# Attention, maxout and bilinear layers on one core: weights of layers three and four in pieces, sums of y per tile

## The chip, the cores and the metric

One core of a Trainium2 chip runs the kernel. The metric is the device time of one execution in microseconds (us); three runs of the kernel before gave a median of 562.81 us (562.11 to 563.57). The engines are PE (matmuls; PEld is its weight load), DVE, ACT, POOL and SP, which here only issues DMAs.

## The reference

Three stages follow each other. The first is attention for 2 batches, 8 heads, 768 positions and 64 features: every query sees the keys within 15 positions and, beside them, 24 block summaries of the sequence.

```python
k_sum = k.reshape(B, H, nb, block, D).max(axis=3)      # block = 32
v_sum = v.reshape(B, H, nb, block, D).mean(axis=3)
scores_l = np.where(abs(pos_q - pos_k) < 16, scale * q @ k.T, -1e9)
scores_s = scale * q @ k_sum.T + log(block)
a = softmax(concat(scores_l, scores_s))
x = a @ concat(v, v_sum)                               # 1536 tokens x 512
h = maximum(maximum(x @ w1, x @ w2), x @ w3)           # layer one, 768 wide
y = h @ w_out                                          # layer two, 512 wide
out = ((y @ w_a) * (y @ w_b)) @ w_out2                 # layers three and four, 1536 wide
```

## The kernel before

The tokens are cut into four chunks of 384, `c` = 0 to 3; chunks 0 and 1 are the first batch, 2 and 3 the second. PE works in pairs of numbers: every operand is split into a rounded part and a remainder (`split`, L513, for activations; `w_parts`, L449, for weights), and a product is three matmuls (`mm3`, L508).

Weights come as 64-bit words in tiles of 128x512. For each, `w_load` (L415) issues a DMA on SP, `w_round` (L429) builds a 32-bit float with two ACT operations, a shift and an or on DVE (L445, L446) and an add on POOL (L447), and `w_split` (L455) makes the two parts with an ACT copy (L451) and a subtraction (L452, on DVE in this stage). Layer three multiplies 2x2 blocks by a seven-product scheme (`PRODUCTS`, L51). So for a pair of its tiles `w_split` also makes four half-width sums on DVE (L467 to L470) and splits two tiles of sums `s` and one quarter tile; and the activations need sums too, the T operands, which `sums_of` (L568) makes from the blocks of y with differences on DVE (`diff`, L581) and a copy and a subtraction for each operand (L578, L579). For chunks 2 and 3 `halves` (L562) calls it behind every second tile of y.

Layers one and two run chunk by chunk (`layers12`); attention of the second batch is laced into them. Then `layers34` runs `order34`: a0, b0, a1, o0, b1, a2, o1 and so on, with a and b the two factors of layer three for 256 features (`layer3`, 14 steps of six matmuls, seven products for each batch) and o layer four (`layer4`, 12 steps of six matmuls). Each step ends in a PSUM bank: qb, qg and qd in layer three, po in layer four, two buffers of each. Banks are emptied a step later by `evac`: ACT copies (L624, L632), adds on DVE (L634, L640), a multiply on DVE (L638) or POOL (L641), then a split into hg (L514 ACT, L515 DVE); in layer four an add on DVE (L681).

`weights(most)` (L480) traces up to `most` whole tiles' work for the next matrices as far as `fits` (L476) has room: room comes back when a layer's products are done (`w_freed`). At the end of the kernel it is called once for each step of `layers34`.

```python
for _ in layers34():
    weights(2)
```

Who runs when: a planner orders each engine's instructions by a simulated timeline, in which work traced earlier goes first among what is ready. `tc.issue_after(ins)` makes every instruction that the block traces on the engine of `ins` follow `ins` in that engine's queue; other engines' instructions are not bound. `mark[0]` is the last DVE instruction of that use. SP alone keeps the order in which its DMAs were traced (L80).

Of the kernel before, what the change touches and what calls it, by code (L numbers as in the profile page):

```python
# [9 lines left out]
F32 = mybir.dt.float32  # L10
# [4 lines left out]
AF = mybir.ActivationFunctionType  # L15
# [4 lines left out]
P = 128  # L20
# [32 lines left out]

W64, W32, WBUFS, QB, FB, SM, GB, BANKS = (4, 3), (4, 3), (24, 10), 4, (8, 2), 2, (12, 9), (2, 2, 1, 2, 2)

GATE, ROOM, SUMS, EARLY34 = (2, 3), 16, (46, 48, 50, 52), 6
LEAD, TURN, ERA0, ASKS, AHEAD, PRE, TURNS = 5, (11, 2, 2), 8, (3, 4, 5, 7, 9), (4, 1), 3, ((6, N1 - 6, 6, 4, 4, 8, N1 - 8, 4, 12), (24, 34), (34, 44))

# [10 lines left out]
def attention_then_maxout_then_bilinear(ctx: ExitStack, tc: tile.TileContext, qt, kt, vt, vwin, wall, const, out):  # L77
# [351 lines left out]
    def w_round(q):  # L429


        r = w64_t.pop(q).bitcast(U32).rearrange("p (n t) -> p n t", t=2)
        lw, hw = r[:, :, 0], r[:, :, 1]
        to = hw.bitcast(F32)
        if q < N12 + EARLY34:

            to = ps_c.tile([P, 512], F32, tag="c", name="psw")
        if BIAS_DVE[era(q)][q % 3]:
            V.tensor_scalar(to, hw.bitcast(F32), 2.0 ** -112, None, ALU.mult)
        else:  # L440
            A.activation(to, hw.bitcast(F32), AF.Copy, scale=2.0 ** -112)
        hw = to.bitcast(U32)
        A.activation(lw.bitcast(I32), lw, AF.Copy, scale=2.0 ** -29)  # L443
        w32_t[q] = w = w32_p.tile([P, 512], F32, tag=f"w32{q < N12}", name="w32", bufs=W32[q >= N12])
        V.tensor_scalar(w.bitcast(U32), hw, 3, None, ALU.logical_shift_left)  # L445
        V.scalar_tensor_tensor(w.bitcast(U32), hw, 0x80000000, w.bitcast(U32), ALU.bitwise_and, ALU.bitwise_or)  # L446
        G.tensor_tensor(w.bitcast(I32), w.bitcast(I32), lw.bitcast(I32), ALU.add)  # L447

    def w_parts(r, eng, tag="w34", n=512):  # L449
        w = w_p.tile([P, 2, n], F32R, tag=tag, name="wt", bufs=2 if n < 512 else WBUFS[tag != "w"])  # L450
# [4 lines left out]
    def w_split(q):  # L455
        kind, n, i = kinds[q]
        eng = V if SPLIT_DVE[era(q)][q % 3] else G
        if kind in ("w", "o"):
            w_t[q] = w_parts(w32_t.pop(q), eng, "w" if kind == "w" else "w34")
        elif i == 0:  # L460
            w = w_parts(w32_t[q], eng)
            w_t[kind, n] = {"A11": (w, 0), "A12": (w, 256)}
        else:
            w0, w1 = w32_t.pop(q - 1), w32_t.pop(q)
            (a11, a12), (a21, a22) = ((w[:, 0:256], w[:, 256:512]) for w in (w0, w1))
            s12, s34 = (w32_p.tile([P, 512], F32, tag=f"s{i}", name="s", bufs=1) for i in range(2))
            V.tensor_tensor(s12[:, 0:256], a21, a22, ALU.add)  # L467
            V.tensor_tensor(s12[:, 256:512], s12[:, 0:256], a11, ALU.subtract)
            V.tensor_tensor(s34[:, 0:256], a11, a21, ALU.subtract)
            V.tensor_tensor(s34[:, 256:512], a12, s12[:, 256:512], ALU.subtract)  # L470
            s12, s34, a22 = w_parts(s12, eng), w_parts(s34, eng), w_parts(a22, eng, "wb", 256)
            w_t[kind, n].update(S1=(s12, 0), S2=(s12, 256), S3=(s34, 0), S4=(s34, 256), A22=(a22, 0))

    w_at, w_done, w_freed, w_room = [0, 0, 0], 0, 0, 0

    def fits(n):  # L476

        return n <= N12 or n - w_freed <= ROOM and n - max(N12, w_freed) <= WBUFS[1]

    def weights(most):  # L480

        nonlocal w_done, w_room
        for _ in range(most):
            if w_done == len(seq) or not fits(w_room + room[w_done]) or w_done == N12 and not gate:
                return
            w_room += room[w_done]
            w_done += 1
            ahead = min(AHEAD[0] + 2 * (w_done < ERA0 + 4), W64[w_done + AHEAD[0] > N12] - 2 * (w_done >= ERA0 + 4))
            for n, (step, more) in enumerate(((w_load, ahead), (w_round, AHEAD[1]), (w_split, 0))):
                while w_at[n] < min(w_done + more, len(seq) if gate else N12):  # L490
                    step(w_at[n])
                    w_at[n] += 1


    late = []
# [66 lines left out]
    def halves(c, m, ps):  # L562

        A.activation(ys[c][:, m], ps, AF.Copy)
        if c >= 2 and m % 2:
            sums_of(c, m)

    def sums_of(c, m):  # L568

        b, j = divmod(c, 2)  # L570
        (b11, b21), (b12, b22) = ((y[:, 0:2], y[:, 2:4]) for y in (ys[2 * b], ys[2 * b + j]))

        def op(name, src):
            names = next(x for x in (("B11", "B21"), ("T1", "T2", "T3", "B22", "T4")) if name in x) if b == 0 else (name,)
            if name == names[0]:
                both[b, names] = t_p.tile([P, len(names), 2, 2, MAXT * P], F32R, tag=names[0] + str(b), name="yt", bufs=1)
            ops[b, name] = t = both[b, names][:, names.index(name)]
            A.activation(t[:, 0], src, AF.Copy)  # L578
            V.tensor_tensor(t[:, 1], src, t[:, 0], ALU.subtract)  # L579

        def diff(tag, x, y):  # L581
            t = y_p.tile([P, 2, MAXT * P], F32, tag=tag, name="yd")
            V.tensor_tensor(t, x, y, ALU.subtract)
            return t

        if j == 0:
            op(("B11", "B21")[m // 2], (b11, b21)[m // 2])
        elif m == 1:
            t1 = sums[b] = diff("t1", b12, b11)
            op("T1", t1)  # L590
        else:
            t2 = diff("t2", b22, sums[b])
            op("T2", t2)
            op("T3", diff("t3", b22, b12))
            op("B22", b22)
            op("T4", diff("t3", b21, t2))

    sums = {}

# [3 lines left out]
    def layer3(kind, n, cs):  # L603

        nonlocal w_freed
        ws = w_t[kind, n]
        ps, kept = {}, {}
        each = [(i, b) for i in range(7) for b in range(B)]
        if (kind, n) in (order34[0], order34[-2]):
            each.sort(key=lambda x: x[1])  # L610
        for i, b in each:
            w, y, bank_ = PRODUCTS[i]
            first = (b, bank_) not in ps
            if first:
                ps[b, bank_] = ps_m.tile([P, 512], F32, tag=f"q{bank_}", name=f"q{bank_}")[:, 0:MAXT * P]
            (wt, o), to = ws[w], ps[b, bank_]
            for k in range(2):
                mm3(to, wt, o + k * P, ops[b, y][:, :, k], first and k == 0, k == 1, not first)
            flush()

            def evac(i=i, b=b, to=to):
                def keep(name):
                    kept[b, name] = t = half(name)
                    A.activation(t, to, AF.Copy)  # L624

                def result(f, j, x):

                    c = 2 * b + j
                    if kind == "a":
                        cs[c, f] = t = half("ca")  # L630
                        if x is None:
                            A.activation(t, to, AF.Copy)  # L632
                        else:
                            V.tensor_tensor(t, to, x, ALU.add)  # L634
                        return
                    t = half("t")
                    if x is None:
                        V.tensor_tensor(t, to, cs[c, f], ALU.mult)  # L638
                    else:
                        V.tensor_tensor(t, to, x, ALU.add)  # L640
                        G.tensor_tensor(t, t, cs[c, f], ALU.mult)  # L641
                    gs[n, c, f] = g = hg_p.tile([P, 2, MAXT * P], F32R, tag="g", name="hg", bufs=GB[1])
                    split(g, t, V)

                if i in (0, 1, 2):
                    keep(("s1", "m5", "u2")[i])
                elif i == 3:
                    result(0, 0, kept[b, "s1"])
                elif i == 4:
                    result(1, 1, kept[b, "m5"])  # L650
                elif i == 5:
                    result(0, 1, kept[b, "u2"])
                else:
                    result(1, 0, None)

            late.append(evac)
            yield
        w_freed += 3
# [3 lines left out]
    def layer4(n, q):  # L662
        nonlocal w_freed
        for c in range(NCH):
            for i in range(CHUNKS[c][2]):
                ps = bank("po")
                for f in range(2):
                    w, g = w_t[q + f], gs[n, c, f][:, :, i * P:(i + 1) * P]
                    T.matmul(ps, g[:, 0], w[:, 0], start=(f == 0), stop=False)  # L669
                    T.matmul(ps, g[:, 0], w[:, 1], start=False, stop=False)  # L670
# [3 lines left out]
                def evac(c=c, i=i, ps=ps):  # L674
# [3 lines left out]
                            acc.update({(c, i): sums[:, c, i] for c in range(NCH) for i in range(MAXT)})  # L678
                        A.activation(acc[c, i], ps, AF.Copy)
                    else:  # L680
                        V.tensor_tensor(acc[c, i], ps, acc[c, i], ALU.add)  # L681
                    if n == NG - 1:
                        r0 = (CHUNKS[c][0] * NT + CHUNKS[c][1] + i) * P
                        nc.sync.dma_start(out=out[r0:r0 + P, :], in_=acc[c, i])
# [52 lines left out]
            done += 1  # L737
    next(dense[-1], None)
    for _ in layers34():
        weights(2)  # L740
    flush()


# [54 lines left out]
```

## Time and profile before

| | |
|---|---|
| median of three runs | 562.81 us |
| the profiled execution's own time | 561.15 us |
| its span | 559.3 us |
| PE busy | 543.4 us (97%) |
| PEld busy | 513.6 us (92%) |
| DVE busy | 376.6 us (67%) |
| ACT busy | 278.0 us (50%) |
| POOL busy | 200.8 us (36%) |

The page of the profile gives busy time by engine, the chain that ended last, and groups of instructions by line. Times in the trace count from the start of the span. The opening (attention of the first batch) takes the first 32 us, layers one and two with attention of the second batch run to 285, layers three and four to 555. Idle time of an engine is put down to the instruction that ended it.

### The profile page before, as it was taken

How to read it: one execution, taken by the hardware profiler on the slowest of the kernel's cores; microseconds unless marked ns; L12 is line 12 of the kernel's file. 1: busy time of each engine (PE TensorE's matmuls, PEld its weight loads, DVE VectorE, ACT ScalarE, POOL GpSimd, SP SyncE). 2: the span in 40 equal slices, each digit the busy share in tenths (PEclk: the TensorE clock that was granted, in tenths of full speed). 3: DMA queues.
4: the chain of work that ended last, by engine and by line, in shares of the span. 5: the costliest groups of instructions: out<-in, count | busy, mean ns of one | idle time of the engine just before them, and what ended most of it. 6: DMA issues, size and time to landing. Idle time of an engine off the chain costs nothing.

```text
span 559.3 us, 9056 instructions
## 1 busy us (share of the span) xinstructions
PE 543.4 (97%) x3374; PEld 513.6 (92%) x3374; DVE 376.6 (67%) x781; ACT 278.0 (50%) x667; POOL 200.8 (36%) x177
## 2 busy tenths in 40 slices
PE   8899999999999999999997999999999999999997
PEld 7889999999999999999997899899899989999985
DVE  5798956964433622839869766866977987773374
ACT  4799765666442413525665656534544453341220
POOL 4389996542110111503604322513413332320030
PEclk9999999999999999999999999999999999999999
DMA  8992473833100020312321222122023120000005
GB/s 315 350 269 84 157 249 119 301 113 111 38 1 2 1 97 16 110 42 76 114 75 39 75 77 76 39 76 79 35 76 114 38 77 37 1 0 1 1 32 194
DMA packets 16987, 51.81 MB, mean 93 GB/s; under 512 B 2096, under 2 KB 2480, under 8 KB 16944
## 3 DMA queue, kind: packets, MB, share of 16 engines
q1 hardware_dynamic: 16944, 51.25, 27.4%
q8 instruction: 26, 0.43, 0.3%
q14 instruction: 17, 0.14, 0.1%
HBM read 48.09 MB, written 3.15 MB: 92 GB/s over the span
## 4 chain that ended last, share of the span: by engine, by line
PE 77%; DVE 12%; DMA 4%; ACT 3%; issue 2%; POOL 2%; SPq 0%; POOLq 0%; DVEq 0%; ACTq 0%
PE ph L511 24%; PE qb L511 13%; PE py L511 9%; PE qg L511 5%; PE po L671 5%; PE po L670 5%; PE po L669 5%; PE qd L511 3%; PE ps L250 3%; DVE wt L452 2%; DVE hg L515 2%; DMA w<-wall 2%; PE psv L305 2%; PE pst L286 1%; DVE t L640 1%
## 5 line engine op out<-in xcount | busy, mean ns | idle before, releaser
L511 PE MATMUL ph<-x,wt 128*128 128x384 f32 x864 | 156.2, 336 | 0.1
L511 PEld LDWEIGHTS ph<-x,wt 128*128 128x128 f32 x864 | 149.2, 188 | 0.7 <-DVE x L515 0.5
L447 POOL TENSOR_TENSOR w<-w,w 128x512 int32<-128x512 int32 x60 | 83.0, 1388 | 154.7 <-DVE w L446 78.0
L511 PE MATMUL qb<-yt,wt 128*128 128x384 f32 x576 | 112.9, 336 | 5.5 <-DVE t L640 2.9
L511 PEld LDWEIGHTS qb<-yt,wt 128*128 128x128 f32 x576 | 101.6, 188 | 10.8 <-DVE t L640 3.3
L514 ACT ACTIVATE hg<-t 128x384 fp32r<-128x384 f32 x72 | 37.0, 522 | 81.2 <-DVE t L538 41.5
L641 POOL TENSOR_TENSOR t<-t,ca 128x384 f32<-128x384 f32 x36 | 42.8, 1201 | 85.4 <-DVE t L640 83.0
L681 DVE TENSOR_TENSOR acc<-po,acc 128x512 f32<-128x512 f32 x60 | 40.8, 686 | 27.5 <-PE po L671 27.4
L511 PE MATMUL qg<-yt,wt 128*128 128x384 f32 x288 | 58.0, 336 | 0.5 <-DVE t L640 0.5
L670 PE MATMUL po<-wt,hg 128*128 128x512 f32 x144 | 56.7, 394 | 0.0
L669 PE MATMUL po<-wt,hg 128*128 128x512 f32 x144 | 56.2, 390 | 0.5 <-ACT hg L514 0.5
L671 PE MATMUL po<-wt,hg 128*128 128x512 f32 x144 | 56.2, 396 | 0.2 <-DVE hg L515 0.2
L511 PE MATMUL py<-hg,wt 128*128 128x384 f32 x288 | 55.2, 340 | 0.0
L511 PEld LDWEIGHTS qg<-yt,wt 128*128 128x128 f32 x288 | 50.6, 188 | 2.8 <-DVE t L640 1.0
L538 DVE TENSOR_TENSOR t<-ph,t 128x384 f32<-128x384 f32 x48 | 26.6, 554 | 37.1 <-PE ph L511 31.1
L511 PEld LDWEIGHTS py<-hg,wt 128*128 128x128 f32 x288 | 49.6, 188 | 0.1
L257 ACT ACTIVATE s<-s,nm 128x120 f32<-128x120 f32 x96 | 37.1, 390 | 22.0 <-DVE nm L256 21.3
L451 ACT ACTIVATE wt<-w 128x512 fp32r<-128x512 f32 (+1 forms) x60 | 35.0, 584 | 18.7 <-PE qb L511 12.8
L452 DVE TENSOR_TENSOR wt<-w,wt 128x512 fp32r<-128x512 f32 (+1 forms) x44 | 32.4, 737 | 16.2 <-ACT wt L451 16.2
L515 DVE TENSOR_TENSOR hg<-t,hg 128x384 fp32r<-128x384 f32 x48 | 40.6, 856 | 3.8 <-ACT hg L514 3.8
L515 POOL TENSOR_TENSOR hg<-t,hg 128x384 fp32r<-128x384 f32 x24 | 26.1, 1091 | 46.7 <-ACT hg L514 45.7
L443 ACT ACTIVATE w<-w 128x512 int32<-128x512 uint32 x60 | 39.3, 668 | 0.5 <-DMA w<-wall 0.5
(80 smaller groups left out, 776.7 us busy)
## 6 DMA issues: line engine op xcount, KB each, us to landing
w<-wall SPq DMA_DIRECT2D x60, 512.0 KB, 3.3
q<-qt SPq DMA_DIRECT2D x15, 384.0 KB, 6.7
row<-kt SPq DMA_DIRECT2D x8, 416.0 KB, 5.8
full<-vt SPq DMA_DIRECT2D x8, 384.0 KB, 6.4
out<-acc SPq DMA_DIRECT2D x12, 256.0 KB, 2.0
v<-vwin SPq DMA_DIRECT2D x12, 192.0 KB, 6.7
v<-vwin SPq DMA_DIRECT2D x12, 96.0 KB, 6.8
q<-qt SPq DMA_DIRECT2D x1, 256.0 KB, 4.4
```

The costliest lines, as they stand in the source:

```text
L257: A.activation(s[:, a], s[:, a], AF.Exp, bias=nm[:, a:a + 1], scale=-1.0, accum_out=sm[:, a:a + 1])
L443: A.activation(lw.bitcast(I32), lw, AF.Copy, scale=2.0 ** -29)
L447: G.tensor_tensor(w.bitcast(I32), w.bitcast(I32), lw.bitcast(I32), ALU.add)
L452: eng.tensor_tensor(w[:, 1], r, w[:, 0], ALU.subtract)
L511: T.matmul(ps, w[:, i, o:o + P], x[:, j], start=first and n == 0, stop=last and n == 2, skip_group_check=more)
L514: A.activation(dst[:, 0], src, AF.Copy)
L515: eng.tensor_tensor(dst[:, 1], src, dst[:, 0], ALU.subtract)
L641: G.tensor_tensor(t, t, cs[c, f], ALU.mult)
L669: T.matmul(ps, g[:, 0], w[:, 0], start=(f == 0), stop=False)
L670: T.matmul(ps, g[:, 0], w[:, 1], start=False, stop=False)
L671: T.matmul(ps, g[:, 1], w[:, 0], start=False, stop=(f == 1))
L681: V.tensor_tensor(acc[c, i], ps, acc[c, i], ALU.add)
```

## The change

The work on weights becomes a generator, cut into pieces by `yield`: two for a rounding, one for a plain split, five for the second tile of a pair. `pieces(most)` runs that many pieces, `weights(most)` still runs whole tiles, and `made` runs pieces until a tile that a product needs has been traced. After each step of layers three and four one piece is traced, behind `mark[0]`, and the adds that empty a bank (L634, L640, L681) now set `mark[0]`. For chunk 3 `halves` calls `sums_of` behind every tile of y, for half of the block (128x384 in place of 128x768), with temporaries of its own for each batch. Three buffer counts change: six tiles in place of four for loaded weights of layers one and two (with the loads asked for further ahead through `ahead`), nine in place of eight for keys and values of the first batch, one in place of two for those of the second.

```diff
@@ -53,14 +53,14 @@
-W64, W32, WBUFS, QB, FB, SM, GB, BANKS = (4, 3), (4, 3), (24, 10), 4, (8, 2), 2, (12, 9), (2, 2, 1, 2, 2)
+W64, W32, WBUFS, QB, FB, SM, GB, BANKS = (6, 3), (4, 3), (24, 10), 4, (9, 1), 2, (12, 9), (2, 2, 1, 2, 2)
 GATE, ROOM, SUMS, EARLY34 = (2, 3), 16, (46, 48, 50, 52), 6
-LEAD, TURN, ERA0, ASKS, AHEAD, PRE, TURNS = 5, (11, 2, 2), 8, (3, 4, 5, 7, 9), (4, 1), 3, ((6, N1 - 6, 6, 4, 4, 8, N1 - 8, 4, 12), (24, 34), (34, 44))
+PIECES, LEAD, TURN, ERA0, ASKS, AHEAD, PRE, TURNS = 1, 5, (11, 2, 2), 8, (3, 4, 5, 7, 9), (4, 1), 3, ((6, N1 - 6, 6, 4, 4, 8, N1 - 8, 4, 12), (24, 34), (34, 44))
@@ -443,8 +443,10 @@
         A.activation(lw.bitcast(I32), lw, AF.Copy, scale=2.0 ** -29)
         w32_t[q] = w = w32_p.tile([P, 512], F32, tag=f"w32{q < N12}", name="w32", bufs=W32[q >= N12])
         V.tensor_scalar(w.bitcast(U32), hw, 3, None, ALU.logical_shift_left)
+        yield
         V.scalar_tensor_tensor(w.bitcast(U32), hw, 0x80000000, w.bitcast(U32), ALU.bitwise_and, ALU.bitwise_or)
         G.tensor_tensor(w.bitcast(I32), w.bitcast(I32), lw.bitcast(I32), ALU.add)
+        yield
     def w_parts(r, eng, tag="w34", n=512):
         w = w_p.tile([P, 2, n], F32R, tag=tag, name="wt", bufs=2 if n < 512 else WBUFS[tag != "w"])
@@ -457,19 +459,29 @@
         eng = V if SPLIT_DVE[era(q)][q % 3] else G
         if kind in ("w", "o"):
             w_t[q] = w_parts(w32_t.pop(q), eng, "w" if kind == "w" else "w34")
+            yield
         elif i == 0:
             w = w_parts(w32_t[q], eng)
             w_t[kind, n] = {"A11": (w, 0), "A12": (w, 256)}
+            yield
         else:
             w0, w1 = w32_t.pop(q - 1), w32_t.pop(q)
             (a11, a12), (a21, a22) = ((w[:, 0:256], w[:, 256:512]) for w in (w0, w1))
             s12, s34 = (w32_p.tile([P, 512], F32, tag=f"s{i}", name="s", bufs=1) for i in range(2))
             V.tensor_tensor(s12[:, 0:256], a21, a22, ALU.add)
             V.tensor_tensor(s12[:, 256:512], s12[:, 0:256], a11, ALU.subtract)
+            yield
+            s1 = w_parts(s12, eng)
+            w_t[kind, n].update(S1=(s1, 0), S2=(s1, 256))
+            yield
             V.tensor_tensor(s34[:, 0:256], a11, a21, ALU.subtract)
             V.tensor_tensor(s34[:, 256:512], a12, s12[:, 256:512], ALU.subtract)
-            s12, s34, a22 = w_parts(s12, eng), w_parts(s34, eng), w_parts(a22, eng, "wb", 256)
-            w_t[kind, n].update(S1=(s12, 0), S2=(s12, 256), S3=(s34, 0), S4=(s34, 256), A22=(a22, 0))
+            yield
+            s3 = w_parts(s34, eng)
+            w_t[kind, n].update(S3=(s3, 0), S4=(s3, 256))
+            yield
+            w_t[kind, n].update(A22=(w_parts(a22, eng, "wb", 256), 0))
+            yield
     w_at, w_done, w_freed, w_room = [0, 0, 0], 0, 0, 0
@@ -477,19 +489,42 @@
         return n <= N12 or n - w_freed <= ROOM and n - max(N12, w_freed) <= WBUFS[1]
-    def weights(most):
+    def work():
+
+        ahead = min(AHEAD[0] + 2 * (w_done < ERA0 + 4), W64[w_done + AHEAD[0] > N12] - 2 * (w_done >= ERA0 + 4))
+        for n, (step, more) in enumerate(((w_load, ahead), (w_round, AHEAD[1]), (w_split, 0))):
+            while w_at[n] < min(w_done + more, len(seq) if gate else N12):
+                w_at[n] += 1
+                yield from step(w_at[n] - 1) or ()
+
+    begun = [iter(())]
+
+    def pieces(most):
         nonlocal w_done, w_room
-        for _ in range(most):
+        while most:
+            for _ in begun[0]:
+                most -= 1
+                if not most:
+                    return True
             if w_done == len(seq) or not fits(w_room + room[w_done]) or w_done == N12 and not gate:
-                return
+                return False
             w_room += room[w_done]
             w_done += 1
-            ahead = min(AHEAD[0] + 2 * (w_done < ERA0 + 4), W64[w_done + AHEAD[0] > N12] - 2 * (w_done >= ERA0 + 4))
-            for n, (step, more) in enumerate(((w_load, ahead), (w_round, AHEAD[1]), (w_split, 0))):
-                while w_at[n] < min(w_done + more, len(seq) if gate else N12):
-                    step(w_at[n])
-                    w_at[n] += 1
+            begun[0] = work()
+
+    def weights(most):
+
+        for _ in range(most):
+            if not pieces(1):
+                return
+            for _ in begun[0]:
+                pass
+
+    def made(kind, n, tile_):
+
+        while not (tile_ in w_t.get((kind, n), ()) if kind in "ab" else n in w_t):
+            assert pieces(1)
     late = []
@@ -562,38 +597,40 @@
     def halves(c, m, ps):
         A.activation(ys[c][:, m], ps, AF.Copy)
-        if c >= 2 and m % 2:
+        if c == 3:
+            sums_of(c, m, m % 2, m % 2 + 1)
+        elif c == 2 and m % 2:
             sums_of(c, m)
-    def sums_of(c, m):
+    def sums_of(c, m, k0=0, k1=2):
         b, j = divmod(c, 2)
-        (b11, b21), (b12, b22) = ((y[:, 0:2], y[:, 2:4]) for y in (ys[2 * b], ys[2 * b + j]))
+        (b11, b21), (b12, b22) = ((y[:, k0:k1], y[:, 2 + k0:2 + k1]) for y in (ys[2 * b], ys[2 * b + j]))
         def op(name, src):
             names = next(x for x in (("B11", "B21"), ("T1", "T2", "T3", "B22", "T4")) if name in x) if b == 0 else (name,)
-            if name == names[0]:
+            if name == names[0] and k0 == 0:
                 both[b, names] = t_p.tile([P, len(names), 2, 2, MAXT * P], F32R, tag=names[0] + str(b), name="yt", bufs=1)
             ops[b, name] = t = both[b, names][:, names.index(name)]
-            A.activation(t[:, 0], src, AF.Copy)
-            V.tensor_tensor(t[:, 1], src, t[:, 0], ALU.subtract)
+            A.activation(t[:, 0, k0:k1], src, AF.Copy)
+            V.tensor_tensor(t[:, 1, k0:k1], src, t[:, 0, k0:k1], ALU.subtract)
         def diff(tag, x, y):
-            t = y_p.tile([P, 2, MAXT * P], F32, tag=tag, name="yd")
+            t = y_p.tile([P, k1 - k0, MAXT * P], F32, tag=f"{tag}{b}{k0 * (tag == 't1')}", name="yd")
             V.tensor_tensor(t, x, y, ALU.subtract)
             return t
         if j == 0:
             op(("B11", "B21")[m // 2], (b11, b21)[m // 2])
-        elif m == 1:
-            t1 = sums[b] = diff("t1", b12, b11)
+        elif m < 2:
+            t1 = sums[b, k0] = diff("t1", b12, b11)
             op("T1", t1)
         else:
-            t2 = diff("t2", b22, sums[b])
+            t2 = diff("t2", b22, sums[b, k0])
             op("T2", t2)
             op("T3", diff("t3", b22, b12))
             op("B22", b22)
-            op("T4", diff("t3", b21, t2))
+            op("T4", diff("t4" if b else "t3", b21, t2))
     sums = {}
@@ -603,7 +640,6 @@
     def layer3(kind, n, cs):
         nonlocal w_freed
-        ws = w_t[kind, n]
         ps, kept = {}, {}
         each = [(i, b) for i in range(7) for b in range(B)]
         if (kind, n) in (order34[0], order34[-2]):
@@ -613,7 +649,8 @@
             first = (b, bank_) not in ps
             if first:
                 ps[b, bank_] = ps_m.tile([P, 512], F32, tag=f"q{bank_}", name=f"q{bank_}")[:, 0:MAXT * P]
-            (wt, o), to = ws[w], ps[b, bank_]
+            made(kind, n, w)
+            (wt, o), to = w_t[kind, n][w], ps[b, bank_]
             for k in range(2):
                 mm3(to, wt, o + k * P, ops[b, y][:, :, k], first and k == 0, k == 1, not first)
             flush()
@@ -631,13 +668,13 @@
                         if x is None:
                             A.activation(t, to, AF.Copy)
                         else:
-                            V.tensor_tensor(t, to, x, ALU.add)
+                            mark[0] = V.tensor_tensor(t, to, x, ALU.add).ins
                         return
                     t = half("t")
                     if x is None:
                         V.tensor_tensor(t, to, cs[c, f], ALU.mult)
                     else:
-                        V.tensor_tensor(t, to, x, ALU.add)
+                        mark[0] = V.tensor_tensor(t, to, x, ALU.add).ins
                         G.tensor_tensor(t, t, cs[c, f], ALU.mult)
                     gs[n, c, f] = g = hg_p.tile([P, 2, MAXT * P], F32R, tag="g", name="hg", bufs=GB[1])
                     split(g, t, V)
@@ -665,6 +702,7 @@
             for i in range(CHUNKS[c][2]):
                 ps = bank("po")
                 for f in range(2):
+                    made("o", q + f, None)
                     w, g = w_t[q + f], gs[n, c, f][:, :, i * P:(i + 1) * P]
                     T.matmul(ps, g[:, 0], w[:, 0], start=(f == 0), stop=False)
                     T.matmul(ps, g[:, 0], w[:, 1], start=False, stop=False)
@@ -678,7 +716,7 @@
                             acc.update({(c, i): sums[:, c, i] for c in range(NCH) for i in range(MAXT)})
                         A.activation(acc[c, i], ps, AF.Copy)
                     else:
-                        V.tensor_tensor(acc[c, i], ps, acc[c, i], ALU.add)
+                        mark[0] = V.tensor_tensor(acc[c, i], ps, acc[c, i], ALU.add).ins
                     if n == NG - 1:
                         r0 = (CHUNKS[c][0] * NT + CHUNKS[c][1] + i) * P
                         nc.sync.dma_start(out=out[r0:r0 + P, :], in_=acc[c, i])
@@ -737,7 +775,8 @@
             done += 1
     next(dense[-1], None)
     for _ in layers34():
-        weights(2)
+        with tc.issue_after(mark[0]):
+            pieces(PIECES)
     flush()
```

## Rows read from the trace of the kernel before

**Rows 1.** The page: the first section, and one group of the fifth.
```profile
PE 543.4 (97%) x3374; PEld 513.6 (92%) x3374; DVE 376.6 (67%) x781; ACT 278.0 (50%) x667; POOL 200.8 (36%) x177
...
L511 PE MATMUL qb<-yt,wt 128*128 128x384 f32 x576 | 112.9, 336 | 5.5 <-DVE t L640 2.9
```
**Rows 2.** Busy time by stretch: PE, PEld, DVE, ACT, POOL (instructions), granted clock, DMA share, GB/s.
```profile
262.00:285.00 23.00, 23.00 (x134) 23.00 (x134) 17.98 (x27) 14.39 (x27) 10.27 (x8) 1.00 0.30 101
285.00:317.00 32.00, 27.32 (x148) 25.13 (x147) 30.20 (x44) 19.57 (x39) 12.46 (x9) 1.00 0.12 45
300.00:317.00 17.00, 12.90 (x68) 11.29 (x67) 17.00 (x25) 11.06 (x23) 9.81 (x8) 1.00 0.18 65
330.00:536.00 206.00, 204.45 (x1062) 188.71 (x1062) 144.48 (x244) 88.89 (x180) 58.38 (x48) 1.00 0.13 47
536.00:555.60 19.60, 18.97 (x85) 15.36 (x83) 14.85 (x25) 3.04 (x7) 4.01 (x4) 1.00 0.36 134
```
**Rows 3.** Waits of PE, 285 to 560: us in total, times, longest us.
```profile
PE qb L511 <- DVE t L640: 2.9, 1, 2.9
PE qb L511 <- DVE t L638: 2.0, 4, 0.9
```
**Rows 4.** Waits of PE, 330 to 536.
```profile
PE qb L511 <- DVE t L638: 1.0, 3, 0.5
```
**Rows 5.** Timeline of PE, 262 to 330: start us, length us, count, idle before.
```profile
301.01 2.24 PE L511 MATMUL qb<-yt,wt 128*128 128x384 f32 x12
306.20 1.33 PE L511 MATMUL qb<-yt,wt 128*128 128x384 f32 x6 [2.95 <-DVE t L640]
```
**Rows 6.** Timeline of DVE, 278 to 317.
```profile
299.27 0.54 DVE L640 TENSOR_TENSOR t<-qb,m 128x384 f32<-128x384 f32 x1
...
303.39 0.68 DVE L452 TENSOR_TENSOR wt<-w,wt 128x512 fp32r<-128x512 f32 x1
...
304.80 0.42 DVE L445 TENSOR_SCALAR w<-w 128x512 uint32<-128x512 uint32 x1
...
305.60 0.55 DVE L640 TENSOR_TENSOR t<-qb,m 128x384 f32<-128x384 f32 x1
```
**Rows 7.** Stretch 292 to 317, DVE's instructions with w alone: length, busy.
```profile
292.00:317.00 25.00, 11.82 (x16) 1.00 0.12 44
```
**Rows 8.** Groups of DVE, 330 to 525: busy us, mean ns, idle before.
```profile
L681 DVE TENSOR_TENSOR acc<-po,acc 128x512 f32<-128x512 f32 x44 | 29.9, 686 | 17.1 <-PE po L671 17.0
...
L446 DVE SCALAR_TENSOR_TENSOR w<-w,w 128x512 uint32<-128x512 uint32 x20 | 14.4, 721 | 0.2
```
**Rows 9.** Waits of DVE, 285 to 560.
```profile
DVE wt L452 <- ACT wt L451: 20.4, 13, 3.7
```
**Rows 10.** Timeline of DVE, 278 to 317, the sums of y.
```profile
285.94 0.96 DVE L583 TENSOR_TENSOR yd<-y,yd 128x768 f32<-128x768 f32 x1 [0.67 <-ACT y L564]
...
292.16 0.96 DVE L579 TENSOR_TENSOR yt<-yd,yt 128x768 fp32r<-128x768 f32 x1 [0.91 <-ACT yt L578]
```
**Rows 11.** The page, fifth section: ACT's copy of 128x384.
```profile
L514 ACT ACTIVATE hg<-t 128x384 fp32r<-128x384 f32 x72 | 37.0, 522 | 81.2 <-DVE t L538 41.5
```
**Rows 12.** The page, sixth section: DMA issues, KB each, us to landing.
```profile
w<-wall SPq DMA_DIRECT2D x60, 512.0 KB, 3.3
```
**Rows 13.** Timeline of SP's queue, 76 to 205.
```profile
98.59 0.33 SPq L152 DMA_DIRECT2D row<-kt  x1
...
101.62 0.38 SPq L152 DMA_DIRECT2D row<-kt  x1
```
**Rows 14.** PE's instructions on psv, 75 to 200: ns min/median/max, first and last start us.
```profile
L305 PE MATMUL psv<-aT,v x192: 222/222/270, 122.4 to 172.6; 120*64 120x64 f32 x192
```
**Rows 15.** Timeline of DVE, 278 to 317, an or.
```profile
297.19 1.68 DVE L446 SCALAR_TENSOR_TENSOR w<-w,w 128x512 uint32<-128x512 uint32 x1
```
**Rows 16.** Timeline of POOL, 296.5 to 300.
```profile
296.72 1.61 POOL L447 TENSOR_TENSOR w<-w,w 128x512 int32<-128x512 int32 x1 [17.78 <-ACT ca L632]
```
**Rows 17.** Timeline of DVE, 546 to 551, layer four.
```profile
548.72 0.69 DVE L681 TENSOR_TENSOR acc<-po,acc 128x512 f32<-128x512 f32 x1 [0.67 <-PE po L671]
```

## Prediction

> **What bounds the kernel now.** I read the first section of the page, then the table of stretches, then what PE waits for from layer three on, then PE's and DVE's timelines round the longest of these waits. PE is busy 543.4 us, 97% of the span [rows 1], at a granted clock of 1.00 in every stretch below [rows 2]. Of the 15.9 us of idle time 32.00 - 27.32 = 4.68 us lie between 285 and 317, where layer three takes over, 1.55 us from 330 to 536 and 0.63 us from there to 555.6 [rows 2]. The rest is the opening and the end, the last sum and store, which the change leaves as they are.
>
> A busy PE hides part of each gap. 134 matmuls go through in 23.00 us, one per 0.172 us [rows 2], while each is shown 0.336 us long [rows 1]; at a gap the other 0.164 us of the last one count as busy. So the four gaps of 285 to 317 cost 4.68 + 4 x 0.16 = 5.3 us, the four from 330 to 536, three of them waits for L638 [rows 4], 1.55 + 0.66 = 2.2 us, the one behind them 0.8 us. These 8.3 us are what layers three and four can give.
>
> Who is waited for? From 285 on above all a DVE operation that empties a PSUM bank: L640 once for 2.9 us, L638 four times for 2.0 us [rows 3]. At the long one PE's twelve qb products end at 301.01 + 2.24 = 303.25 and PE starts again at 306.20 [rows 5], after the add on qb began at 305.60 [rows 6]. DVE was not idle: it is busy 17.00 of the 17.00 us from 300 to 317 [rows 2]. Among what stood in front of that add are a split of 0.68 us and a shift of 0.42 us [rows 6], weight work for matrices that PE needs only layers later. From 292 to 317 the operations on w alone take 11.82 of 25 us of DVE [rows 7], the splits of s not counted. So the stage is bound by the order on DVE, not by its amount: from 330 to 525 DVE sits 17.1 us idle ahead of L681 [rows 8].
>
> **Weights, one piece per step.** Before, a step at which room is free traces up to two whole matrices, and the planner may put their DVE operations into any hole. Now one piece per step is traced, and its DVE operations stand behind the last add that emptied a bank (L634, L640, L681). No DVE work is removed; the same shifts, sums and splits only move. What room allows until layer three starts is the same in both programs. In the 28 steps of b0 and a1 it allows 6 and 10 pieces; by lone durations (0.42 for a shift, a half-width sum or the quarter split, 0.68 for a 512-wide or and split [rows 6]) that is 4 x (0.42 + 0.68) + 5 x 0.68 + 5 x 0.42 = 9.9 us in 28 steps of 6 x 0.172 = 1.03 us, against over 11.82 in 25 us now. An evacuation then finds at most one piece ahead. I let two waits of one piece of 0.68 us stand, 1.4 us: gain 5.3 - 1.4 = 3.9 us. Ends: 5.3 (no wait left) and 0 (the planner puts others in front).
>
> Later, three of the four waits are for L638, the multiply, which does not move the mark, so a piece can still stand before it. I take half of the 2.2 us: gain 1.1, ends 2.2 and 0.
>
> **The added wait.** A piece at the head of DVE's queue may itself wait for ACT or POOL; behind it stand the next adds and the hg splits, and PE waits for those. Its price is DVE's wait for ACT at L452: 20.4 us in 13 waits, 1.57 each [rows 9], of which PE feels little now. Nearest to what PE would feel is the 1.0 us of L638 [rows 4]: I charge 0.9 us, ends 0 and rival D. Deadlines do not press: per n there are 10 + 10 + 6 = 26 pieces for 14 + 14 + 12 = 40 steps, and room is given a whole layer ahead of a matrix's first product. The loads of these weights stay three deep on SP, in the old order.
>
> **Sums of chunk 3 per tile.** Nine DVE operations of 128x768 become eighteen of 128x384. At 0.96 [rows 10] and 0.54 us [rows 6] that is 18 x 0.54 - 9 x 0.96 = +1.1 us of DVE, less where successive ones overlap; ACT's copies double in number at 0.522 us each [rows 11], with ACT half idle. But half of the work behind the last y tile now runs before it. DVE has it in hand from 285.94 to 292.16 + 0.96 = 293.12 [rows 10]; seven half operations and two ACT copies are 7 x 0.54 + 2 x 0.52 = 4.8 us, so the last operand is ready 2.4 us sooner. Among the four gaps only the smallest ones, under 1 us each, can hang on that, and they are counted above: b0's products for the first batch fill the rest. I book 0, ends -1.1 and +1.1 us. The buffer of its own for the fourth difference takes its wait away inside the same 2.4 us.
>
> **Buffers and loads.** W64[0] 6 for 4 lets layer-one weights be asked for two matrices earlier, past q, v and k loads on SP's queue. One such load takes 3.3 us to land [rows 12]; that bounds it both ways. I book 0, since both kinds are fetched a group or more ahead of their use. FB[1] 1 for 2 lets keys and values of batch two share one buffer: each row load now waits for the means of the pair before, each full load for the maxima of its own row. One such turn takes 101.62 - 98.59 = 3.0 us today [rows 13]; seven more of them from 98.59 on end near 120. The products with the values run from 122.4 to 172.6 in eight groups [rows 14], 6.3 us each, so the fourth pair is wanted at 141: 20 us of cover. Booked 0; if the cover fails, a DVE reduction at the head of the queue holds evacuations for one turn, +3 us.
>
> **Sum.** -3.9 - 1.1 + 0.9 = -4.1 us against the profiled execution's own 561.15 us: 557.0. That execution lies 1.7 us below the median of the runs shown, 562.81; against the median the forecast is **558.7 us**.
>
> **One rule weighed.** At 297.19 the or L446, both inputs in SBUF, took 1.68 us [rows 15] beside POOL's add from 296.72 to 298.33 [rows 16], where the form has 0.72 us in the mean [rows 8]; the add L640 at 299.27, one input in PSUM, took its usual 0.54 [rows 6]. The Trainium skill, SBUF — State Buffer, section "Who interferes with whom", has it that a VectorE instruction with two SBUF inputs contends with a GpSimd instruction that reads SBUF, and that the later one is held for the other's whole length. The trace agrees. It speaks against this change: the add behind which a piece is queued is also the one that releases POOL's multiply L641, so the two start together. What this would do is rival D.
>
> **Rivals.**
> A, the forecast: 558.7, own range 556 to 561.
> B, everything goes: all 8.3 us vanish, 562.8 - 8.3 = 554.5. For it: the evacuations by DVE are 4.9 us of PE's idle [rows 3]. Against: L638 and the hg splits are not protected.
> C, the edit does not do what it says: only DVE's weight work is held, while ACT's copies and POOL's adds may still be hoisted, and the planner fills the holes with hg splits, so the 3.1 us wait comes back in another place. Then the later 1.1 us and the added 0.9 remain: 562.6. For it: DVE has up to 25 - 11.8 = 13.2 us of other work in that window, crowded behind the sums of y.
> D, slower: pieces collide with POOL. In layer four twelve steps carry ten to twelve pieces. A step is 0.69 + 0.67 = 1.36 us long, of which DVE is idle 0.67 [rows 17]; a piece of 0.68 fits, one of 1.68 overshoots by a us. With the second bank taking up 0.3 of it, each collided piece costs 0.7 + 0.16 us. It decides from 4.1 / 0.86, five such pieces in the whole stage; I take two in each of four layer fours: 562.8 - 4.1 + 6.9 = 565.6. For it: the rows of 297. Against: from 330 to 525 the or's mean is 721 ns over twenty [rows 8], so few collide as things are ordered now, with as many POOL adds.
>
> **Chances.** A 0.53, B 0.10, C 0.20, D 0.17. A change of 0.3% (1.7 us) is about what a measurement of this kernel tells from none: faster is A and B, 0.63; within 0.3% is C, 0.20; slower is D, 0.17. The range is 554 to 565.5: it takes in the ends of the large terms and leaves out the tail of B and half of D.
>
> **What would show it.** Right: between the last py product and layer three's steady state only gaps under 1 us; the DVE operations L445 to L470 thin out from 292 to 306 and come back behind L634, L640 and L681; the last L579 done within 5 us of the last y; span near 555 with PE's busy time near 543 as before. Wrong: a gap of 2 us or more for L640 stays (C); L446 and L452 average over 0.9 us from 330 on, with PE gaps at po (D); PE gaps between 75 and 170 (the single buffer).

## The result: slower by 1%

The changed kernel takes 568.17 us in the median of four runs (566.89 to 569.63), the one before 562.70 in the same session: a ratio of 1.0101, 95% interval 1.0087 to 1.0116. The forecast was 558.7, with a range that ended at 565.5. The profiled execution has a span of 565.1 us, 5.8 more than before.

The table of stretches of the changed kernel answers to [rows 2]: length, then PE, PEld, DVE, ACT and POOL busy, granted clock, DMA share, GB/s.

```profile
262.00:285.00 23.00, 23.00 (x134) 23.00 (x133) 14.82 (x25) 14.10 (x28) 7.12 (x6) 1.00 0.15 50
285.00:317.00 32.00, 27.88 (x149) 25.26 (x148) 25.72 (x44) 17.58 (x37) 9.57 (x8) 1.00 0.14 50
330.00:536.00 206.00, 199.14 (x1029) 184.33 (x1028) 147.76 (x252) 93.22 (x185) 61.08 (x49) 0.99 0.16 54
536.00:561.40 25.40, 25.26 (x118) 21.29 (x116) 17.13 (x29) 4.17 (x8) 5.28 (x5) 1.00 0.28 104
```

Up to 285 PE is as busy as before, though less weight work is done by then: of the ors on the weights of layers three and four (L447, before L446) two have run by 285 and five by 317, where it had been four and eight. From 285 to 317 PE idles 4.12 us where it was 4.68: the expected 3.9 us did not come. From 330 to 536 it idles 206.00 - 199.14 = 6.86 us where it was 1.55. The last stretch gains half a us. What PE waits for from 285 to 560 (us in total, times, longest) answers to [rows 3]; L675 is the multiply that was L638, L677 the add that was L640, L661 an ACT copy out of a bank.

```profile
PE qb L546 <- DVE t L675: 5.7, 4, 2.6
PE qg L546 <- ACT m L661: 3.1, 2, 1.6
PE qb L546 <- DVE t L677: 0.7, 1, 0.7
PE qd L546 <- DVE t L677: 0.6, 1, 0.6
```

The waits for the add have shrunk as forecast: 2.9 us on qb and 0.5 on qg have become 0.7 on qb and 0.6 on qd. The waits for the multiply, which the new code does not mark, have grown from 2.0 to 5.7, and 3.1 us of waits for ACT's copy out of qg are new. PE's timeline shows them where a layer b ends: here b2, b3 and b4 (three answers; start us, length us, count, idle before).

```profile
401.00 2.25 PE L546 MATMUL qg<-yt,wt 128*128 128x384 f32 x12
404.87 1.31 PE L546 MATMUL qb<-yt,wt 128*128 128x384 f32 x6 [1.63 <-DVE t L675]
```

```profile
448.77 2.25 PE L546 MATMUL qg<-yt,wt 128*128 128x384 f32 x12
452.52 1.32 PE L546 MATMUL qg<-yt,wt 128*128 128x384 f32 x6 [1.50 <-ACT m L661]
454.99 1.96 PE L546 MATMUL qb<-yt,wt 128*128 128x384 f32 x6 [1.15 <-DVE t L675]
456.74 2.12 PE L546 MATMUL qg<-yt,wt 128*128 128x384 f32 x6
```

```profile
499.41 2.25 PE L546 MATMUL qg<-yt,wt 128*128 128x384 f32 x12
504.24 1.33 PE L546 MATMUL qb<-yt,wt 128*128 128x384 f32 x6 [2.58 <-DVE t L675]
```

The end of b0, inside 285 to 317, has two more, 1.56 us for the ACT copy and 0.39 for the multiply. At the ends of b1 and b5 PE waits for neither.

DVE's timeline at the end of b3 shows what stood in front of the multiply, POOL's what ran beside it.

```profile
447.58 0.54 DVE L677 TENSOR_TENSOR t<-qg,u 128x384 f32<-128x384 f32 x1
448.05 0.77 DVE L445 TENSOR_SCALAR w<-w 128x512 uint32<-128x512 uint32 x1
448.74 1.23 DVE L471 TENSOR_TENSOR s<-w 128x256 f32<-128x256 f32 x1
449.90 1.24 DVE L477 TENSOR_TENSOR s<-w,w 128x256 f32<-128x256 f32 x1
451.06 0.54 DVE L550 TENSOR_TENSOR hg<-t,hg 128x384 fp32r<-128x384 f32 x1
451.53 0.68 DVE L447 SCALAR_TENSOR_TENSOR w<-w,w 128x512 uint32<-128x512 uint32 x1
452.13 0.41 DVE L472 TENSOR_TENSOR s<-s,w 128x256 f32<-128x256 f32 x1
452.46 1.66 DVE L550 TENSOR_TENSOR hg<-t,hg 128x384 fp32r<-128x384 f32 x1
454.05 0.41 DVE L454 TENSOR_TENSOR wt<-w,wt 128x256 fp32r<-128x256 f32 x1
454.39 0.55 DVE L675 TENSOR_TENSOR t<-qb,ca 128x384 f32<-128x384 f32 x1
```

```profile
447.21 3.65 POOL L678 TENSOR_TENSOR t<-t,ca 128x384 f32<-128x384 f32 x3
452.34 1.37 POOL L448 TENSOR_TENSOR w<-w,w 128x512 int32<-128x512 int32 x1 [1.49 <-ACT hg L549]
```

From the last add of b3 to its first multiply pass 454.39 - 447.58 = 6.8 us, with six weight operations in front of it. In the kernel before, the same place has none, only a split of hg:

```profile
449.64 0.55 DVE L640 TENSOR_TENSOR t<-qg,u 128x384 f32<-128x384 f32 x1
450.10 1.18 DVE L515 TENSOR_TENSOR hg<-t,hg 128x384 fp32r<-128x384 f32 x1
451.21 1.01 DVE L638 TENSOR_TENSOR t<-qb,ca 128x384 f32<-128x384 f32 x2
```

The pile is not the same everywhere: two weight operations stand there at the end of b2 and four at b4, beside splits of hg, and at b1 five go through in 4.8 us and PE loses nothing. ACT, whose queue the mark does not bind, waited 1.53 us for POOL's multiply at the end of b3 and ran three weight operations before the copy out of qg at 451.99.

The code says why weight work gathers there. `mark[0]` moves only at an add. After b's last add come two multiplies, which set no mark, and in the next layer a ACT keeps the first three products of each batch; its first add is traced after half of its 14 steps. So all pieces of these steps are held behind b's last add, every one of them is free to go once that add is done, and the planner puts them into what it takes for a hole, in front of the multiplies. That is the theory T1 of the experiments, a stale mark.

### The profile page after: what moved, and what is told of

It reads as the page before. It is cut to its first block, busy times and chain, and to the rows that moved or that the text cites. A ratio compares the mean times of both kernels' runs of the same rounds, so it can differ in the third digit from the quotient of the medians.

```text
span 565.1 us, 8987 instructions
## 1 busy us (share of the span) xinstructions
PE 544.5 (96%) x3374; PEld 515.4 (91%) x3374; DVE 375.3 (66%) x790; ACT 280.5 (50%) x672; POOL 199.6 (35%) x177
## 4 chain that ended last, share of the span: by engine, by line
PE 83%; DVE 9%; DMA 3%; ACT 2%; issue 1%; POOL 1%; SPq 0%; ACTq 0%
PE ph L546 27%; PE qb L546 15%; PE py L546 9%; PE qg L546 6%; PE po L709 5%; PE po L708 5%; PE po L707 5%; PE qd L546 3%; PE ps L250 3%; DVE hg L550 2%; PE psv L305 2%; PE pst L286 2%; DMA full<-vt 1%; DVE w L447 1%; DVE wt L454 1%; DMA q<-qt 1%
## 5 line engine op out<-in xcount | busy, mean ns | idle before, releaser
L546 PE MATMUL qb<-yt,wt 128*128 128x384 f32 x576 | 116.3, 338 | 7.3 <-DVE t L675 5.7
L546 PE MATMUL qg<-yt,wt 128*128 128x384 f32 x288 | 60.0, 340 | 3.1 <-ACT m L661 3.1
L678 POOL TENSOR_TENSOR t<-t,ca 128x384 f32<-128x384 f32 x36 | 41.0, 1156 | 50.5 <-DVE t L677 50.3
L550 DVE TENSOR_TENSOR hg<-t,hg 128x384 fp32r<-128x384 f32 x48 | 35.5, 752 | 8.3 <-ACT hg L549 8.3
L275 POOL TENSOR_TENSOR s<-s,r 128x720 f32<-128x720 f32 x16 | 22.2, 1389 | 44.7 <-DVE r L273 33.4
```

Source lines behind the costliest of these rows:

```text
L546: T.matmul(ps, w[:, i, o:o + P], x[:, j], start=first and n == 0, stop=last and n == 2, skip_group_check=more)
L550: eng.tensor_tensor(dst[:, 1], src, dst[:, 0], ALU.subtract)
```

## The experiments

Each kernel was timed in three rounds against the kernel before, which had medians of 562.23, 561.91 and 562.39 us in the three groups. "No sums" means `halves` and `sums_of` as before the change.

**Which part is it?** `e1_pieces`, no sums (the edit of `halves`; `sums_of` goes back with it):

```diff
-        if c == 3:
-            sums_of(c, m, m % 2, m % 2 + 1)
-        elif c == 2 and m % 2:
+        if c >= 2 and m % 2:
             sums_of(c, m)
```

> The change without the sums per tile: pieces behind the mark, and the new buffer counts. Theory T1 (stale mark): layer b ends with two multiplies that empty qb and set no mark, so the pieces traced in the first half of the next layer a all stand behind b's last add, that is in front of the multiplies, where POOL's multiply slows them; this is in this kernel unchanged, so 568 us (567 to 569.5) with gaps of 1.6 us or more at the ends of b2, b3 and b4. Rival T2 (the sums per tile, or the buffers with them, cost the time): 562.7, or if the buffers do, 568 without those gaps.

567.76 us, ratio 1.0096 (1.0068 to 1.0125). The waits for the multiply are there, 5.3 us in three (its PE waits, 330 to 560):

```profile
PE qb L546 <- DVE t L673: 5.3, 3, 2.6
PE qg L546 <- ACT m L659: 1.7, 1, 1.7
```

`e2_sums` is the other half, the kernel before with the new `halves` and `sums_of` and the new buffer counts.

> The kernel before with the sums per tile and the new buffer counts, and without the pieces. T1: no more than 0.3% from before, 562.7 (561.5 to 564), gaps at the ends of the layers b as before, 0.4 to 0.9 us. T2: 568.

561.76 us, 0.9994 (0.9985 to 1.0003). T2 falls: the pieces alone make the kernel slower. The sums and buffers cost and give nothing, either by themselves or, as below, with the defect mended.

**Is it the mark?** `e4_mark_mult`:

```diff
-                        V.tensor_tensor(t, to, cs[c, f], ALU.mult)
+                        mark[0] = V.tensor_tensor(t, to, cs[c, f], ALU.mult).ins
```

> The changed kernel, in which the multiply that empties qb sets the mark too; one line. T1: the gaps at the ends of b2 to b4 (1.9 + 3.2 + 2.9 us) and the 1.6 us at the lower clock behind b3 go, in all 9.5 us: 559 us (557.5 to 562). Rival T3 (weights come too late, one piece per step is too slow, or DVE has too much to do at the end of b in any order): 567 to 569.

558.02 us, 0.9931 (0.9917 to 0.9946): one line takes back 10 us, and the kernel is now faster than the one before. PE no longer waits for a multiply from 285 on, nor for the copy out of qg; between b3's last add and its multiplies stands only one hg split:

```profile
444.48 0.54 DVE L677 TENSOR_TENSOR t<-qg,u 128x384 f32<-128x384 f32 x1
444.95 1.57 DVE L550 TENSOR_TENSOR hg<-t,hg 128x384 fp32r<-128x384 f32 x1
446.44 1.01 DVE L675 TENSOR_TENSOR t<-qb,ca 128x384 f32<-128x384 f32 x2
```

Idle of 285 to 317 falls too, to 32.00 - 29.81 = 2.19 us. T3 (too slow a pace, too much work at the end of b) falls with it. A single new wait of 1.9 us stands in a3: ACT waits at the head of its queue for a weight, and the bank copy is behind it. Behind this wait the clock fell (last section).

```profile
456.54 0.67 ACT L441 ACTIVATE w<-w 128x512 f32<-128x512 f32 x1 [2.63 <-DMA w<-wall]
457.10 0.66 ACT L443 ACTIVATE w<-w 128x512 int32<-128x512 uint32 x1
457.65 0.85 ACT L661 ACTIVATE u<-qb 128x384 f32<-128x384 f32 x2
```

`e5_no_hold` keeps the pieces and drops the hold (no sums, buffers as before):

```diff
-        with tc.issue_after(mark[0]):
-            pieces(PIECES)
+        pieces(PIECES)
```

> Pieces one per step, not held behind any mark; buffers and sums as before the change. T1: the weight work may go into earlier holes again and the large gaps at the ends of b2 to b4 are absent: 561 to 564. T3 (the pacing is at fault): 566 or more.

562.42 us, 1.0004 (0.9993 to 1.0016). Pieces without the hold are the kernel before again, its 3.1 us wait for the add at the start of layer three included.

**Why do six short operations cost so much?** `e6_after_no_mult` takes POOL's multiply out of the changed kernel, `e7_before_no_mult` out of the one before:

```diff
-                        G.tensor_tensor(t, t, cs[c, f], ALU.mult)
```

> The changed kernel without POOL's multiply L678, which leaves the product with the other factor out for three of four results; the weight pieces still stand behind the last add and in front of the two DVE multiplies. If the collision with that multiply makes the gaps (a half-width sum of 1.23 us in place of 0.42 at the end of b), they fall under 1 us each: 560 us (558.5 to 562). If the number of pieces in front of the multiplies is enough by itself, gaps of 1.5 us or more stay: 565 or more.

> The kernel before without POOL's multiply L641, as a control for the one above. Collision theory: few weight operations meet the multiply here, so little changes at the ends of the layers b: 561 (559.5 to 563). If taking POOL's multiply away helps any order of DVE alike, by more than 1%: under 557.

`e6`: 555.22 us, 0.9872 (0.9857 to 0.9888). `e7`: 555.32 us, 0.9873 (0.9858 to 0.9889). Without POOL's multiply the change is neutral; with it, it costs 1%. At the end of b3, DVE of `e6` has five of the six weight operations in the order of the changed kernel and one hg split more, and is through in 445.94 - 442.13 = 3.8 us in place of 6.8:

```profile
442.13 0.55 DVE L677 TENSOR_TENSOR t<-qg,u 128x384 f32<-128x384 f32 x1
442.60 0.41 DVE L445 TENSOR_SCALAR w<-w 128x512 uint32<-128x512 uint32 x1
442.93 0.41 DVE L471 TENSOR_TENSOR s<-w 128x256 f32<-128x256 f32 x1
443.27 0.42 DVE L477 TENSOR_TENSOR s<-w,w 128x256 f32<-128x256 f32 x1
443.60 1.02 DVE L550 TENSOR_TENSOR hg<-t,hg 128x384 fp32r<-128x384 f32 x2
444.54 0.68 DVE L447 SCALAR_TENSOR_TENSOR w<-w,w 128x512 uint32<-128x512 uint32 x1
445.14 0.55 DVE L550 TENSOR_TENSOR hg<-t,hg 128x384 fp32r<-128x384 f32 x1
445.61 0.42 DVE L472 TENSOR_TENSOR s<-s,w 128x256 f32<-128x256 f32 x1
445.94 1.02 DVE L675 TENSOR_TENSOR t<-qb,ca 128x384 f32<-128x384 f32 x2
```

So five weight operations in front of the multiplies are harmless at their lone length: PE of `e6` waits at no end of a layer b. In the changed kernel the shift and two sums beside the multiply took 2.0 us more than here; another 1.1 us is the hg split of 1.66, which ran beside POOL's weight add of 452.34 and not beside the multiply. `e6` came out below the range expected for it, and my control missed: I had expected 561 for `e7`. The multiply costs the old order 6.6 us as well (the mean hg split from 330 to 560 falls from 842 to 623 ns without it), so `e7` shows that POOL is expensive here and not that the old order is free of it. Both kernels also lose POOL's time between add and split.

`e10_memset` was to keep that time and take only the reading away:

```diff
-                        G.tensor_tensor(t, t, cs[c, f], ALU.mult)
+                        for _ in range(3):
+                            G.memset(t, 0.0)
```

> The changed kernel in which three memsets of t on POOL stand in place of POOL's multiply L678, so three of four results come out as nothing; POOL is still in the path from the add to the split, but between add and split it reads no SBUF. If the gaps come from DVE's two-input operations waiting for a POOL instruction that reads SBUF, the half-width sum L477 between the last add and the multiply is back at 0.42 us and the gaps at the ends of the layers b under 1 us each: 558 us (555.5 to 561). If POOL's time in the path to the hg splits makes the gaps, or any POOL work holds DVE, gaps of 1.5 us or more stay: 564 or more.

558.50 us, 0.9929 (0.9912 to 0.9946), as the collision has it. At the end of b1 a half-width sum runs beside the memsets (DVE first, then POOL):

```profile
351.02 0.41 DVE L471 TENSOR_TENSOR s<-w 128x256 f32<-128x256 f32 x1
```

```profile
349.57 3.33 POOL L679 MEMSET t<- 128x384 f32 x8 [3.49 <-DVE t L677]
```

The half-width sum's mean falls from 794 ns in the changed kernel (first fence, DVE's groups of 330 to 560) to 417 (second):

```profile
L471 DVE TENSOR_TENSOR s<-w 128x256 f32<-128x256 f32 x7 | 5.6, 794 | 1.8 <-POOL w L448 1.8
```

```profile
L471 DVE TENSOR_TENSOR s<-w 128x256 f32<-128x256 f32 x7 | 2.9, 417 | 1.7 <-POOL w L448 1.7
```

But the planner also moved some of these sums behind a multiply, and two larger gaps are left at the ends of layers b. One of 0.9 us stands at b2's end, where two hg splits took 3.28 us beside POOL's weight adds. One of 1.07 us, over the expected limit of 1 us, stands at b0's end: seven weight operations at their lone length stood in front of the multiply there, so a long enough pile costs something without any collision. So it supports the collision and does not weigh it alone. The Trainium skill, SBUF — State Buffer, section "Who interferes with whom", makes the same difference: a two-input VectorE instruction contends with a GpSimd instruction that reads SBUF, not with one that only writes it. The runs agree, 1.23 us beside the multiply and 0.42 with memsets.

**What is worth keeping?** `e8_fix_no_sums` is `e4` with no sums and the buffers as before.

> Pieces behind the mark with the multiply marked, but the sums of chunk 3 and the buffer counts as before the change. If the sums per tile are worth nothing by themselves: 558.0, as with them (557 to 559.5). If they give back the 2.4 us by which the last operand is earlier: 560 or more.

557.71 us, 0.9915 (0.9900 to 0.9931): the sums per tile are worth nothing.

`e9_fix_two` is `e4` with two pieces per step, `e11_two_no_sums` and `e13_three_no_sums` are `e8` with two and three.

```diff
-PIECES, LEAD, TURN, ERA0, ASKS, AHEAD, PRE, TURNS = 1, 5, ...
+PIECES, LEAD, TURN, ERA0, ASKS, AHEAD, PRE, TURNS = 2, 5, ...
```

> The changed kernel with the multiply marked and two pieces per step. Stale-mark theory: the ends of the layers b stay clear, since all pieces still stand behind a multiply, and the time stays between 556.5 and 560. If the rate of one piece per step matters by itself, two bring the gaps back: 563 or more.

> Two pieces per step, the multiply marked, sums and buffers as before the change. If what two pieces gained (556.3 against 558.0) and what leaving the sums out gained (557.7 against 558.0) are real and add up: 556.0 (555 to 557). If two pieces gained by chance of one order: 557.5 to 559.

> As with two pieces per step, but three; the multiply marked, sums and buffers as before. If more work earlier keeps DVE's later stretches freer: 556 or less. If it crowds the adds of layer four: 558 or more.

556.30 us, 0.9888 (0.9867 to 0.9908); 556.93, 0.9908 (0.9886 to 0.9930); 556.17, 0.9889 (0.9874 to 0.9904). The first lies just below its range. The second lies in its range and yet above the first, so that the two gains add up is not shown. The third decides neither of its alternatives. The intervals of the three overlap, so they are not told apart.

`e12_whole_marked` is `e8` without pieces: whole matrices, held behind a mark that the multiply moves too (no sums, buffers as before).

```diff
         with tc.issue_after(mark[0]):
-            pieces(PIECES)
+            weights(2)
```

> Whole matrices as before, weights(2) at every step, but held behind the mark, the multiply marked; sums and buffers as before. If the mark with the multiply does it and the cutting into pieces adds nothing: 556.5 to 558.5. If pieces are needed, because a whole matrix behind one mark blocks the next evacuations: 561 or more.

555.83 us, 0.9887 (0.9873 to 0.9902), below the range expected and the lowest median of the kernels that leave nothing out, though its interval overlaps with those of `e9`, `e11` and `e13`. PE idles 1.62 and 0.50 us in the two stretches that had 4.68 and 1.55 in [rows 2]:

```profile
285.00:317.00 32.00, 30.38 (x168) 28.91 (x167) 24.86 (x43) 17.85 (x36) 10.12 (x8) 1.00 0.15 50
330.00:536.00 206.00, 205.50 (x1070) 190.33 (x1069) 156.13 (x260) 92.87 (x184) 70.16 (x52) 1.00 0.15 53
```

Cutting the work into pieces is not needed. What pays is the order on DVE: weight work behind the operations that empty a bank, the multiply among them.

## Why the prediction was wrong

**What bounds the kernel** held. With the right order on DVE the two stretches give back 4.1 us of idle time, the median falls by 6.6, and no DVE work was removed. What makes up the rest of the 6.6 was not taken apart.

**Weights, one piece per step: the step that failed.** "An evacuation then finds at most one piece ahead" is false. I counted pieces by the step that traces them and took the mark to move at every step. It stands still from the last add of a layer b to the first add of the next a. Six weight operations stood in front of b3's multiply where I had allowed one of 0.68 us. I had even noted that the multiply moves no mark, and drew from it only that half of 2.2 us would stay: booked as a gain of 1.1 us, it was a loss. Idle from 330 to 536 went up by 6.86 - 1.55 = 5.3 us. In 285 to 317 the gain was 0.6 us of idle in place of 3.9, in part for the same reason: with the multiply marked (`e4`) it is 4.68 - 2.19 = 2.5. The two waits that I let stand there are the 0.62 and 0.65 us for the add, 1.3 us for the booked 1.4.

**The added wait and rival D.** The 0.9 us stood for DVE waiting for ACT at the head of its queue. Nothing of it shows: this wait of the weight splits fell from 20.4 to 3.3 us. The mechanism of D was right and its place was not: the pieces met POOL's multiply not in layer four, where the bank adds move the mark at every step and PE shows no gap, but behind the last add of layer three, where three multiplies in a row were running; part of the loss there came beside POOL's weight adds. D's price for one collided piece, a us, fits 1.23 for 0.42. I gave it 0.17 because the mean of the or was low in the trace of before; that mean came from an order which the change was about to replace.

**Sums of chunk 3.** The last operand was ready at 289.45 in place of 293.12, 3.7 us sooner where I had 2.4 (DVE's timeline of the changed kernel):

```profile
287.96 1.49 DVE L616 TENSOR_TENSOR yt<-yd,yt 128x384 fp32r<-128x384 f32 x3
293.91 0.56 DVE L671 TENSOR_TENSOR ca<-qb,m 128x384 f32<-128x384 f32 x1 [4.46 <-PE qb L546]
```

DVE then waits 4.46 us for PE: nothing hung on it. Booked 0, measured 0 (`e2`, `e8`).

**Buffers and loads.** Booked 0, and PE's last matmul of y starts at 285.0 us in both kernels.

**Rivals.** For the changed kernel D's 565.6 came nearest, with its collisions in the other place. B's 554.5 is near the mended order (`e12`, 555.8). C was half right: the long wait for the add went, and idle time came back elsewhere in the same stretch (4.12 for 4.68 us), for the most part through weight work behind b0's last add and not through hg splits.

## What to carry to other kernels

Where work is held behind "the last instruction that did X", list every instruction that does X and look for the longest stretch of program in which the mark does not move; all work traced there is set free at one point. Before holding work behind an instruction, look at what else that instruction releases on an engine that gets in its way. And judge such a change by the order it makes, not by durations averaged over the order it replaces.

## What the runs showed of the hardware

Behind the two waits at the end of b3 the granted clock was 0.53 from 455.2 to 458.2, close to the lower of TensorE's two levels, 1.2 of 2.4 GHz:

```profile
455.20:458.20 3.00, 3.00 (x11) 3.00 (x11) 3.00 (x7) 3.00 (x7) 0.00 (x0) 0.53 0.34 137
```

Twelve matmuls took 458.66 - 454.99 = 3.67 us in place of 12 x 0.172 = 2.07: 1.6 of the 5.8 us. The clock did not fall each time that PE had waited so long. In `e1` nearly the same two waits at the same place left the pace as it was:

```profile
452.40 1.31 PE L546 MATMUL qg<-yt,wt 128*128 128x384 f32 x6 [1.66 <-ACT m L659]
454.85 1.31 PE L546 MATMUL qb<-yt,wt 128*128 128x384 f32 x6 [1.14 <-DVE t L673]
```

In `e4` the clock fell behind a single wait of 1.88 us:

```profile
459.40:462.00 2.60, 2.60 (x8) 2.11 (x7) 1.16 (x2) 1.25 (x2) 0.00 (x0) 0.50 0.00 0
```

Behind a single wait of 3.06 us in `e5` it was 0.52 from 307.4 to 310.4; behind single waits of 2.58 us (at 504 in the changed kernel) and 2.95 us (at 306 in the kernel before) PE kept its pace. So a wait can cost more than its length, and neither the length nor the number of the waits tells here when; no run was made to settle it.

Executions of one kernel differ in this, too. The changed kernel's four runs had mean granted clocks of 0.997, 0.997, 0.990 and 0.993; the profiled one is the fastest, 566.89 us. Those of `e1` go from 565.17 us at 0.999, the profiled one, to 568.94 at 0.990. In `e4` the profiled run, 0.997, is the slowest with 559.15 us; the other three, at 1.000, took 557.35 to 558.10. So the medians hold some loss at the lower clock behind the waits that the traces shown do not; how much is not shown.
